# First MoE in three blocks of 768 tokens in place of six of 384, its sums packed into six PSUM banks

## The chip, the cores and the metric

One core of a Trainium2 chip runs the whole program. TensorE (PE in the profile) multiplies matrices and writes its results into PSUM, a memory of eight banks of 512 float32 columns on 128 partitions; VectorE (DVE), ScalarE (ACT) and GpSimd (POOL) do the elementwise work, SyncE (SP) issues the transfers. POOL does not touch PSUM in this kernel. The metric is the device time of one launch in microseconds (us); what is compared is the median of several runs.

## What is computed

A block-causal attention over q, k, v (4 batches, 8 heads, 576 positions, 64 wide) gives x of 2304 tokens x 512. Two MoE layers follow, in float32:

```
h = x @ w_in                     # 512 -> 2048
x2 = (h * cos(h)) @ w_out        # 2048 -> 512, the first MoE

logits = x2 @ w_gate             # 8 experts
P = exp(logits - logits.max())
for _ in range(8):               # rows, then columns, normalized
    P /= P.sum(1, keepdims=True) + 1e-09
    P /= P.sum(0, keepdims=True) + 1e-09
    P *= N / E
out = sum over e of P[:, e] * (relu(x2 @ w1[e]) @ w2[e])   # 512 -> 1024 -> 512
```

## The kernel before

Every float32 operand x is split into a part that TensorE's fp32r format holds (`xh`, by a copy that rounds) and the rest (`xl`, by a subtraction); a product is three matmuls, high by high, high by low, low by high (`mm3`, L473). The order of the instructions is written out by hand: each engine runs its own instructions in the order in which the code emits them, and semaphores make one wait for another.

**First MoE, `moe1`.** A unit (L191) is a pair of a block of 384 tokens and one of 16 chunks `f` of 128 hidden columns: six blocks, 96 units. The weights of a chunk are 512 + 512 columns (`raw[f]`), and they are split anew for each unit: `wsplit(n, 0)` makes `jh`, `jl` of `w_in`, `wsplit(n, 1)` those of `w_out`, the high part on ACT (L65), the low on POOL (L68). `h_unit` issues the 12 hidden matmuls into a PSUM tile `h` (pool `psh`, three banks) and the DVE's range reduction `ki`, `r`; `sine` runs on ACT; `g_unit` multiplies on the DVE (`g`), copies on ACT (`hh`) and subtracts on the DVE (`hl`). `o_unit(n - 2)` issues the 12 output matmuls of the unit two back into four PSUM tiles `acc` (pool `psa`, four banks, 384 of 512 columns used) that add up over the 16 chunks. At the last chunk of a block, ACT copies each to `xh` (L704) and the DVE writes the rest to `xl` (L705).

Between the units other work is put in. In the first 16, three steps each of `conv_gen` convert the last of the weights (they come as float64; DVE L92, L111, L115, L122, ACT L98, L99, POOL L124), and `leftover` finishes the last head of the attention. After blocks 1 to 5 have begun, `logits` of the block before runs on TensorE (eight matmuls into the one bank of pool `psm`) and `logits_t` turns it. From unit 35 on, `tprep` (L590) makes sums and differences of x2 on the DVE, and `steps` prepares the second MoE's first weights in the last block.

**Second MoE.** 96 groups, each of 768 tokens and a pair of chunks of an expert. In a group, `open_group` starts products `hx` and `hy`, and the loop goes on with `hz` (pool `psh`) and six output tiles `y`, also called `acc`. A product named S2 adds onto `hx` once ACT has copied it to `c`. `gate(n)` runs the next n of the list `gating`: logits of block 5, its turning, the maximum (`gmax`), `start_p` with the exponential, and eight column steps `cols`, each a matmul on sums and nine small DVE operations. P is first wanted at the second expert, in group 5.

Of the kernel before, what the change touches and what calls it, by code (L numbers as in the profile page):

```python
# [22 lines left out]
NC = DM // 128  # L23
# [17 lines left out]
def attention_moe_kernel(ctx: ExitStack, tc: tile.TileContext, qk, v, w_a, gate, w_b, out):  # L41
# [425 lines left out]
    with tc.manual_schedule():  # L467
        conv_gen, leftover = attention()
        psh = ctx.enter_context(tc.tile_pool(name="psh", bufs=3, space=PSUM))
        psa = ctx.enter_context(tc.tile_pool(name="psa", bufs=4, space=PSUM))  # L470
        psm = ctx.enter_context(tc.tile_pool(name="psm", bufs=1, space=PSUM))
# [6 lines left out]
        def hidden(wh, wl, blk):  # L478
            ps = psh.tile([128, TB], F32, tag="h", name="h")
            t0 = blk * TB  # L480
# [18 lines left out]
        def logits(blk):  # L499
            t0 = blk * TB  # L500
            ps = psm.tile([2 * NE, TB], F32, tag="m", name="plt")
# [6 lines left out]
        def logits_t(blk):  # L508
            ps = psm.tile([128, TT, 2 * NE], F32, tag="m", name="plg")
# [140 lines left out]
        def moe1():  # L650
            nonlocal th, tl
            with tc.tile_pool(name="m1", bufs=2) as p:
                wj, G = {}, {}
                units = [(blk, f) for blk in range(NB) for f in range(F1)]

                def hl_tiles():
                    return (p.tile([128, TB], F32R, tag="hh", name="hh", bufs=3),
                            p.tile([128, TB], F32R, tag="hl", name="hl", bufs=3))

                def wsplit(n, part, lo_eng=nc.gpsimd):  # L660
                    if 0 <= n < len(units):
                        hi = p.tile([128, DM], F32R, tag=f"jh{part}", name="jh", bufs=3 - part)
                        lo = p.tile([128, DM], F32R, tag=f"jl{part}", name="jl", bufs=3 - part)
# [3 lines left out]
                def h_unit(n):  # L667
                    ps = hidden(*wj.pop((n, 0)), units[n][0])
                    ki = p.tile([128, TB], I32, tag="ki", name="ki", bufs=1)
                    r = p.tile([128, TB], F32, tag="r", name="r")  # L670
                    g = p.tile([128, TB], F32, tag="g", name="g")
# [4 lines left out]
                    return ps, r, g  # L676

                def sine(ps, r, g):
                    nc.scalar.activation(r, r, AF.Sin, bias=half_pi)

                def g_unit(n, fill, ps, r, g):
                    fill[0]()
                    nc.vector.tensor_tensor(out=g, in0=ps, in1=r, op=ALU.mult)
                    G[n] = hl_tiles()
                    nc.scalar.activation(G[n][0], g, AF.Copy)  # L685
                    fill[1]()
                    nc.vector.tensor_tensor(out=G[n][1], in0=g, in1=G[n][0].bitcast(F32), op=ALU.subtract)  # L687
# [3 lines left out]
                def o_unit(n, between):  # L691
                    blk, f = units[n]
                    if f < F1 - 1:
                        between()
                    hh, hl = G.pop(n)
                    wh, wl = wj.pop((n, 1))
                    for m in range(NC):
                        if f == 0:
                            acc[m] = psa.tile([128, DM], F32, tag="a", name="acc")
                        s = slice(m * 128, (m + 1) * 128)  # L700
                        mm3(acc[m][:, 0:TB], wh[:, s], wl[:, s], hh, hl, f == 0, f == F1 - 1)
                        if f == F1 - 1:
                            cols = slice(blk * TB, (blk + 1) * TB)
                            nc.scalar.activation(xh[:, m, cols], acc[m][:, 0:TB], AF.Copy)  # L704
                            nc.vector.tensor_tensor(out=xl[:, m, cols], in0=acc[m][:, 0:TB],  # L705
                                                    in1=xh[:, m, cols].bitcast(F32), op=ALU.subtract)
                            if m == 1:
                                between()

                wsplit(0, 0, nc.vector)  # L710
                wsplit(1, 0, nc.vector)
                wsplit(0, 1)
                gate_prep()
                last = len(units) - F1
                none = lambda: None

                def some(n):
                    for _ in range(n):
# [5 lines left out]
                         13: lambda: w0.v(1, nc.vector), 14: lambda: wload(1)}  # L724
                tgen = None
                for n in range(len(units) + 2):
                    fill = [lambda: some(2), lambda: some(1)] if n < F1 else [none, none]
                    if n == 2 * F1 + 3:
# [3 lines left out]
                    if tgen and n % 2:  # L732
                        fill = [lambda: next(tgen, None), none]
                    between = none
                    if n < len(units):
                        hs = h_unit(n)
                        between = lambda: (sine(*hs), wsplit(n + 2, 0))
                    elif n == len(units) + 1:
                        open_group(0)
                    if n > 1:  # L740
                        o_unit(n - 2, between)
                    else:
                        between()
                    if n < len(units):
                        g_unit(n, fill, *hs)
                        wsplit(n + 1, 1)
# [207 lines left out]
```

## Time and profile before

| | us |
|---|---|
| runs | 2244.49, 2243.87, 2243.08 |
| median | 2243.87 |
| span of the profiled execution | 2242.3 |
| median above that span | 1.6 |
| TensorE busy in the span | 2158.4 (96%) |
| DVE / ACT / POOL busy | 1571.1 / 1020.5 / 1115.1 |
| first MoE: first hidden matmul to last output matmul | 269.3 to 712.0 |

The profile is of one execution. Its page gives busy times by engine and in 40 slices of the span; the trace behind it answers for stretches, lines, waits and single instructions. "PE" is the matmuls, "PEld" the loads of the stationary operand, which overlap them. A matmul's record is longer than the distance to the next one's start, since matmuls are pipelined; that distance is what counts.

### The profile page before, as it was taken

Reading aid. Unit: us, or ns where it says so; the run is one execution under the profiler, and the core shown is the slowest. Engines: PE = TensorE matmul, PEld = TensorE weight load, DVE = VectorE, ACT = ScalarE, POOL = GpSimd, SP = SyncE. Lnnn points to the kernel's source line nnn. Section 1 sums busy time; section 2 is a strip of 40 time slices with the busy share of each in tenths; the row PEclk is TensorE's granted clock in tenths of the full one; section 3 lists DMA queues with packets and bytes.
Section 4 is the critical chain, followed back from the end, with each engine's and each line's share of the span. In section 5 each row is a group of like instructions: output and inputs, shape, how many; then the busy total and the mean of one; then the engine's idle time right before and its main releaser. Section 6 shows DMA issues by size and latency. Waiting matters only on the chain.

```text
span 2242.3 us, 29534 instructions
## 1 busy us (share of the span) xinstructions
PE 2158.4 (96%) x10869; PEld 1910.0 (85%) x10869; DVE 1571.1 (70%) x2477; ACT 1020.5 (46%) x1882; POOL 1115.1 (50%) x928
## 2 busy tenths in 40 slices
PE   7888789999998999999999999999999999999999
PEld 4555589998997888888888888888988888888988
DVE  8888776676666876666676666666676666666665
ACT  5666655555555333433344333433444434333432
POOL 5888785665554334343554434343554434344341
PEclk9999999999999999999999999999999999999999
DMA  5666410000001112121221312121221312121220
GB/s 154 167 165 175 123 34 1 1 1 1 1 19 53 61 57 75 57 76 57 76 64 50 118 61 76 57 76 58 74 69 50 118 57 76 57 76 62 71 73 31
DMA packets 74160, 152.83 MB, mean 68 GB/s; under 512 B 32896, under 2 KB 32896, under 8 KB 74016
## 3 DMA queue, kind: packets, MB, share of 16 engines
q1 hardware_dynamic: 74016, 150.95, 21.7%
q8 instruction: 85, 1.39, 0.3%
q14 instruction: 59, 0.48, 0.1%
HBM read 136.91 MB, written 4.87 MB: 63 GB/s over the span
## 4 chain that ended last, share of the span: by engine, by line
PE 64%; DVE 3%; ACT 1%; issue 0%; ACTq 0%; DVEq 0%
PE acc L474 11%; PE acc L476 11%; PE acc L475 11%; PE hx L476 6%; PE hx L474 6%; PE hx L475 6%; PE hy L474 3%; PE hy L476 3%; PE hy L475 3%; PE hz L474 1%; PE hz L475 1%; PE hz L476 1%; DVE wal L576 0%; ACT hh L810 0%; DVE hl L811 0%; DVE tl L68 0%
## 5 line engine op out<-in xcount | busy, mean ns | idle before, releaser
L585 POOL TENSOR_TENSOR wv<-stg,wv 128x512 fp32r<-128x512 f32 x190 | 335.7, 1788 | 852.7 <-ACT wv L584 852.7
L474 PE MATMUL acc<-wv,hh 128*128 128x512 f32 x1152 | 456.3, 396 | 0.0
L476 PE MATMUL acc<-wv,hl 128*128 128x512 f32 x1152 | 455.6, 395 | 0.0
L475 PE MATMUL acc<-wv,hh 128*128 128x512 f32 x1152 | 454.5, 395 | 0.0
L839 DVE SCALAR_TENSOR_TENSOR oa<-acc,P,oa 128x512 f32<-128x512 f32 x540 | 379.0, 740 | 5.2 <-PE acc L476 4.3
L810 ACT ACTIVATE hh<-c 128x384 fp32r<-128x384 f32 x288 | 151.3, 525 | 409.6 <-DVE c L896 166.0
L68 POOL TENSOR_TENSOR jl<-raw,jh 128x512 fp32r<-128x512 f32 x190 | 253.5, 1344 | 168.5 <-ACT jh L65 166.5
L811 DVE SCALAR_TENSOR_TENSOR hl<-c,hh 128x384 fp32r<-128x384 f32 x288 | 163.9, 569 | 176.4 <-ACT hh L810 176.4
L476 PEld LDWEIGHTS acc<-wv,hl 128*128 128x128 f32 x1152 | 216.0, 187 | 53.7
L475 PEld LDWEIGHTS acc<-wv,hh 128*128 128x128 f32 x1152 | 215.9, 187 | 44.0
L474 PEld LDWEIGHTS acc<-wv,hh 128*128 128x128 f32 x1152 | 216.1, 188 | 43.0
L890 DVE TENSOR_TENSOR c<-hz,c 128x384 f32<-128x384 f32 x96 | 53.4, 556 | 192.0 <-PE hz L476 192.0
L880 ACT ACTIVATE c<-hx 128x384 f32<-128x384 f32 x96 | 47.4, 494 | 282.7 <-PE hx L476 282.7
L576 DVE TENSOR_TENSOR wal<-s,wah 128x1024 fp32r<-128x1024 f32 x96 | 172.2, 1793 | 0.0
L65 ACT ACTIVATE jh<-raw 128x512 fp32r<-128x512 f32 x192 | 119.3, 622 | 99.4 <-PE acc L475 86.7
L476 PE MATMUL h<-xh,jl 128*128 128x384 f32 x384 | 132.2, 344 | 10.3 <-POOL jl L68 10.2
L687 DVE TENSOR_TENSOR hl<-g,hh 128x384 fp32r<-128x384 f32 x96 | 100.7, 1048 | 56.8 <-ACT hh L685 56.8
L474 PE MATMUL h<-xh,jh 128*128 128x384 f32 x384 | 131.6, 343 | 9.1 <-ACT jh L65 8.9
L474 PE MATMUL acc<-hh,jh 128*128 128x384 f32 x384 | 129.4, 337 | 2.2 <-DVE xl L705 1.3
L474 PE MATMUL hy<-xh,wah 128*128 128x384 f32 x384 | 129.2, 337 | 1.3 <-DVE c L896 1.3
L475 PE MATMUL h<-xl,jh 128*128 128x384 f32 x384 | 130.2, 339 | 0.0
L476 PE MATMUL hy<-xh,wal 128*128 128x384 f32 x384 | 129.1, 336 | 0.7 <-DVE wal L576 0.7
(214 smaller groups left out, 5158.4 us busy)
## 6 DMA issues: line engine op xcount, KB each, us to landing
stg<-in_w_b_dram SPq DMA_DIRECT2D x192, 512.0 KB
cw<-in_w_a_dram SPq DMA_DIRECT2D x32, 512.0 KB
st<-in_qk_dram SPq DMA_DIRECT2D x64, 144.0 KB
v<-in_v_dram SPq DMA_DIRECT2D x31, 160.0 KB
tt<-inv SPq DMA_DIRECT2D x32, 144.0 KB
out_dram<-oa SPq DMA_DIRECT2D x18, 256.0 KB
kb<-ka SPq DMA_DIRECT2D x31, 144.0 KB
qb<-qa SPq DMA_DIRECT2D x31, 144.0 KB
```

The costliest lines, as they stand in the source:

```text
L65: nc.scalar.activation(hi, src, AF.Copy)
L68: eng_lo.tensor_tensor(out=lo, in0=src, in1=hi.bitcast(F32), op=ALU.subtract)
L474: nc.tensor.matmul(ps, lh, rh, start=first, stop=False, skip_group_check=go_on)
L475: nc.tensor.matmul(ps, lh, rl, start=False, stop=False, skip_group_check=go_on)
L476: nc.tensor.matmul(ps, ll, rh, start=False, stop=last, skip_group_check=go_on)
L576: eng.tensor_tensor(out=self.al, in0=self.s, in1=self.ah.bitcast(F32), op=ALU.subtract)
L585: eng.tensor_tensor(out=t[:, DM:2 * DM], in0=src, in1=t[:, 0:DM].bitcast(F32), op=ALU.subtract)
L687: nc.vector.tensor_tensor(out=G[n][1], in0=g, in1=G[n][0].bitcast(F32), op=ALU.subtract)
L810: nc.scalar.activation(hh, src, AF.Relu)
L811: nc.vector.scalar_tensor_tensor(out=hl, in0=src, scalar=0.0, in1=hh.bitcast(F32), op0=ALU.max, op1=ALU.subtract)
L839: nc.vector.scalar_tensor_tensor(out=o, in0=acc, scalar=p, in1=o, op0=ALU.mult, op1=ALU.add)
L890: nc.vector.tensor_tensor(out=c[0], in0=z, in1=c[0], op=ALU.add)
```

## The change

The blocks of the first MoE become 768 tokens, so there are 48 units, and each split of a weight chunk serves two half-units of 384 tokens. The hidden matmuls stay 384 columns wide, 24 to a unit, in two PSUM tiles of a pool `psh` of two banks. The output sums of 4 x 768 columns lie in six banks: `PLACE` puts chunk 0 of a pair at bank 0 (512) and the first half of bank 1 (256), chunk 1 at the second half of bank 1 (256) and bank 2 (512). So the output matmuls are 512 and 256 columns wide, and their count and total of columns stay. They are of the unit one back, in two halves of 12; the evictions follow each half at a block's end. `logits` of four of the six old blocks run inside the stage, in a tile of `psh` between the two halves; those of the last two go to the second MoE's gating list, whose calls are placed anew. `tprep` starts at unit 21 of 48 and takes one step a unit. After the stage the six banks become `psm`, `psz` (for `hz`) and `psa`.

```diff
-        psh = ctx.enter_context(tc.tile_pool(name="psh", bufs=3, space=PSUM))
-        psa = ctx.enter_context(tc.tile_pool(name="psa", bufs=4, space=PSUM))
-        psm = ctx.enter_context(tc.tile_pool(name="psm", bufs=1, space=PSUM))
+        psh = ctx.enter_context(tc.tile_pool(name="psh", bufs=2, space=PSUM))
...
-                units = [(blk, f) for blk in range(NB) for f in range(F1)]
+                units = [(blk, f) for blk in range(N // HB) for f in range(F1)]
+                NU = len(units)
+                PLACE = [[(0, 0, 0, 512), (1, 0, 512, 256)], [(1, 256, 0, 256), (2, 0, 256, 512)]]
...
+                    for m in range(2):
+                        s = slice((2 * half + m) * 128, (2 * half + m + 1) * 128)
+                        for i, (w, h) in enumerate(((wh, hh), (wh, hl), (wl, hh))):
+                            for b, at, t0, w_ in PLACE[m]:
+                                nc.tensor.matmul(acc[half, b][:, at:at + w_], w[:, s], h[:, t0:t0 + w_],
...
+                for blk in range(N // HB - 1):
+                    for i, k in ((1, 2 * blk), (4, 2 * blk + 1)):
+                        steps[(blk + 1) * F1 + i - last] = lambda k=k: logits(k, psh, "h")
+                        steps[(blk + 1) * F1 + i + 1 - last] = lambda k=k: logits_t(k, psh, "h")
...
+                        pa = hidden(*w, t0)
+                        ra = reduce_h(pa)
+                        pb = hidden(*w, t0 + TB)
+                        sine(ra)
+                        wsplit(n + 1, 0)
+                        ga = times(pa, ra)
+                        g_hi(n, 0, ga)
+                        rb = reduce_h(pb)
+                        g_lo(n, 0, ga)
+                        wsplit(n, 1)
+                        sine(rb)
+                        some(2)
+                        gb = times(pb, rb)
+                        g_hi(n, 1, gb)
+                        some(1)
+                        g_lo(n, 1, gb)
+                    else:
+                        open_group(0)
+                    if n:
+                        o_part(n - 1, 0)
+                        evacuate(n - 1, 0)
+                    if n - last in steps:
+                        steps[n - last]()
+                    if n:
+                        o_part(n - 1, 1)
+                        evacuate(n - 1, 1)
...
-        gating = [lambda: logits(NB - 1), last_logits, gmax, start_p]
+        gating = [lambda: logits(NB - 2, psm, "m"), lambda: logits_t(NB - 2, psm, "m"),
+                  lambda: logits(NB - 1, psm, "m"), last_logits, gmax, start_p]
...
-                gate(1)
-                z = psh.tile([128, TB], F32, tag="h", name="hz")
+                if g:
+                    gate(1)
+                z = psz.tile([128, TB], F32, tag="z", name="hz")
                 product(g, z, "A12", "B21", True)
+                if g == 0:
+                    gate(1)
...
-            gate(0 if g else 1)
+            if g in (1, 2):
+                gate(1)
```

Three more `gate(1)` for group 0 follow S3, A22 and S4, and the last call, `gate(1 if g else 2)`, becomes `if g: gate(1)`.

The DVE's order in the first MoE, at one unit of the middle. Each row is a line of the kernel, the operation, its output and inputs, the output's size and the engines that it waits for. Before, a unit and the next one's first row:

```order
L672 TENSOR_SCALAR ki<-h 128x384 [waits PE_49]
L674 SCALAR_TENSOR_TENSOR r<-ki,h 128x384 [waits DVE_49]
L683 TENSOR_TENSOR g<-h,r 128x384 [waits Activation_49]
L687 TENSOR_TENSOR hl<-g,hh 128x384 [waits Activation_49]
L672 TENSOR_SCALAR ki<-h 128x384 [waits PE_49]
```

After, a unit of two halves:

```order
L667 TENSOR_SCALAR ki<-h 128x384 [waits PE_49]
L669 SCALAR_TENSOR_TENSOR r<-ki,h 128x384 [waits DVE_49]
L678 TENSOR_TENSOR g<-h,r 128x384 [waits Activation_49]
L667 TENSOR_SCALAR ki<-h 128x384 [waits DVE_49,PE_49]
L669 SCALAR_TENSOR_TENSOR r<-ki,h 128x384 [waits DVE_49]
L686 TENSOR_TENSOR hl<-g,hh 128x384 [waits Activation_49]
L678 TENSOR_TENSOR g<-h,r 128x384 [waits Activation_49]
L686 TENSOR_TENSOR hl<-g,hh 128x384 [waits Activation_49]
```

The second half's `ki` and `r` stand between the first half's `g` and `hl`.

TensorE's output matmuls, the first ones of a unit. Before:

```order
L474 MATMUL acc<-hh,jh 128x384 [waits Activation_49]
L475 MATMUL acc<-hl,jh 128x384 [waits DVE_49]
L476 MATMUL acc<-hh,jl 128x384
L474 MATMUL acc<-hh,jh 128x384
L475 MATMUL acc<-hl,jh 128x384
```

After:

```order
L702 MATMUL acc<-hh,jh 128x512 [waits Activation_49]
L702 MATMUL acc<-hh,jh 128x256
L702 MATMUL acc<-hl,jh 128x512 [waits DVE_49]
L702 MATMUL acc<-hl,jh 128x256
L702 MATMUL acc<-hh,jl 128x512 [waits Pool_49]
L702 MATMUL acc<-hh,jl 128x256
L702 MATMUL acc<-hh,jh 128x256
L702 MATMUL acc<-hh,jh 128x512
```

Each stationary operand now serves two matmuls in a row, 512 and 256 columns wide.

ACT's order where the first MoE ends; `c<-hx` is the copy that the second MoE's first S2 waits for, `wbh` a weight split. Before:

```order
L704 ACTIVATE xh<-acc 128x384 [waits PE_49] x4
L880 ACTIVATE c<-hx 128x384
L560 ACTIVATE wbh<-stg 128x512 [waits DMAHW2_49]
L561 ACTIVATE wbh<-stg 128x256 [waits DMAHW3_49]
L885 ACTIVATE c<-hx 128x384 [waits DVE_49,PE_49,Pool_49]
```

After:

```order
L713 ACTIVATE xh<-acc 128x512 [waits PE_49]
L713 ACTIVATE xh<-acc 128x256 [waits PE_49]
L713 ACTIVATE xh<-acc 128x256 [waits DVE_49]
L713 ACTIVATE xh<-acc 128x512 [waits PE_49] x2
L713 ACTIVATE xh<-acc 128x256 [waits PE_49]
L713 ACTIVATE xh<-acc 128x256 [waits DVE_49]
L713 ACTIVATE xh<-acc 128x512 [waits PE_49]
L904 ACTIVATE c<-hx 128x384
```

Eight copies stand ahead of `c` in place of four, and the second 256-column piece of a bank waits for the DVE, which reads the first.

## Rows read from the trace of the kernel before

**Rows 1.** The page's first part: busy us (share of the span), instructions

```profile
PE 2158.4 (96%) x10869; PEld 1910.0 (85%) x10869; DVE 1571.1 (70%) x2477; ACT 1020.5 (46%) x1882; POOL 1115.1 (50%) x928
```

**Rows 2.** Stretches: length, busy us (count) PE, PEld, DVE, ACT, POOL; clock, DMA share, GB/s

```profile
269.30:346.50 77.20, 69.81 (x360) 66.70 (x361) 58.44 (x88) 42.80 (x74) 58.15 (x40) 0.92 0.11 32
346.50:485.80 139.30, 138.17 (x792) 134.93 (x792) 95.86 (x149) 76.00 (x137) 83.97 (x64) 1.00 0.00 1
485.80:629.70 143.90, 139.93 (x791) 134.59 (x791) 97.91 (x151) 77.40 (x139) 84.00 (x64) 1.00 0.00 1
629.70:707.70 78.00, 73.30 (x410) 69.37 (x409) 54.38 (x83) 40.95 (x74) 43.02 (x32) 1.00 0.13 41
744.80:797.80 53.00, 50.11 (x247) 43.08 (x246) 45.68 (x103) 18.75 (x36) 19.20 (x19) 1.00 0.20 60
797.80:813.50 15.70, 15.70 (x79) 14.07 (x78) 11.89 (x23) 6.25 (x12) 6.01 (x7) 1.00 0.22 65
```

**Rows 3.** Timeline (start, us, instruction): first and last of 25 matmul starts in a row

```profile
419.84 0.33 PE L474 MATMUL h<-xh,jh 128*128 128x384 f32 x1
...
424.00 0.33 PE L474 MATMUL h<-xh,jh 128*128 128x384 f32 x1
```

**Rows 4.** TensorE's waits in the first MoE: total us, times, longest

```profile
PE h L476 <- POOL jl L68: 10.2, 13, 2.4
PE h L474 <- ACT jh L65: 8.9, 4, 4.9
```

**Rows 5.** Timeline of the DVE in block 5: one unit, and a later `hl`

```profile
674.85 0.54 DVE L672 TENSOR_SCALAR ki<-h 128x384 int32<-128x384 f32 x1
...
676.73 0.56 DVE L683 TENSOR_TENSOR g<-h,r 128x384 f32<-128x384 f32 x1 [0.74 <-ACT r L679]
677.88 1.13 DVE L687 TENSOR_TENSOR hl<-g,hh 128x384 fp32r<-128x384 f32 x1 [0.59 <-ACT hh L685]
...
705.05 0.56 DVE L687 TENSOR_TENSOR hl<-g,hh 128x384 fp32r<-128x384 f32 x1 [0.59 <-ACT hh L685]
```

**Rows 6.** Groups on the DVE, 274 to 320 us, conversion (count, busy us, mean ns, idle before)

```profile
L122 DVE SCALAR_TENSOR_TENSOR tla<-cw,tla 128x512 int32<-128x512 int32 x6 | 6.8, 1126 | 0.0
L115 DVE SCALAR_TENSOR_TENSOR raw<-cw,raw 128x512 f32<-128x512 uint16 x5 | 5.6, 1119 | 0.1
...
L92 DVE TENSOR_SCALAR tla<-cw 128x512 int32<-128x512 int32 x5 | 4.0, 801 | 0.0
L111 DVE TENSOR_SCALAR raw<-cw 128x512 int32<-128x512 int32 x5 | 2.7, 533 | 0.0
```

**Rows 7.** Clock: two stretches as in rows 2, and the matmul after a gap

```profile
267.40:274.20 6.80, 4.90 (x15) 4.68 (x16) 3.47 (x7) 2.95 (x4) 2.47 (x2) 0.51 0.00 0
725.00:731.70 6.70, 6.23 (x20) 6.21 (x21) 2.90 (x8) 2.57 (x6) 5.50 (x6) 0.52 0.27 78
...
305.20 0.69 PE L474 MATMUL h<-xh,jh 128*128 128x384 f32 x1 [2.87 <-ACT jh L65]
```

**Rows 8.** Timeline of TensorE: 12 matmuls of 512 columns; two of 256, in the attention

```profile
999.69 0.39 PE L474 MATMUL acc<-wv,hh 128*128 128x512 f32 x1
...
1002.49 0.34 PE L474 MATMUL hx<-xh,wbh 128*128 128x384 f32 x1
...
182.04 0.28 PE L295 MATMUL sr<-qb,kb 128*128 128x256 f32 x1
...
182.28 0.31 PE L295 MATMUL sr<-qb,kb 128*128 128x320 f32 x1
```

**Rows 9.** Timeline, end of group 0: TensorE's wait, and `wal` on the DVE

```profile
725.47 0.58 PE L776 MATMUL pmb<-sm,ones 1*128 1x1 f32 x2 [3.26 <-DVE sm L772]
...
724.01 1.22 DVE L576 TENSOR_TENSOR wal<-s,wah 128x1024 fp32r<-128x1024 f32 x1
```

**Rows 10.** Timeline of TensorE where the first MoE ends: last output matmul, S2

```profile
711.66 0.34 PE L476 MATMUL acc<-hh,jl 128*128 128x384 f32 x1
712.96 0.44 PE L474 MATMUL hx<-th,wah 128*128 128x384 f32 x1 [0.96 <-ACT c L880]
```

More of the change, by code (lines that the diff above doesn't have):

```diff
@@ L689, in moe1, with g_hi, g_lo, o_part @@
+                def g_hi(n, k, g):
+                    nc.scalar.activation(G[n][0][:, k * TB:(k + 1) * TB], g, AF.Copy)
+                def g_lo(n, k, g):
+                    s = slice(k * TB, (k + 1) * TB)
+                    nc.vector.tensor_tensor(out=G[n][1][:, s], in0=g, in1=G[n][0][:, s].bitcast(F32),
+                                            op=ALU.subtract)
                 acc = {}
-                def o_unit(n, between):
+                def o_part(n, half):
                     blk, f = units[n]
[L693 to L708, printed above, removed]
@@ new lines, in o_part @@
+                    hh, hl = G[n]
+                    wh, wl = wj[n, 1]
+                    if f == 0:
+                        for b in range(3):
+                            acc[half, b] = pacc.tile([128, 512], F32, tag=f"a{half}{b}", name="acc")
+                    for m in range(2):
[3 more added lines that the diff above has]
+                                nc.tensor.matmul(acc[half, b][:, at:at + w_], w[:, s], h[:, t0:t0 + w_],
+                                                 start=f == 0 and i == 0 and at == 0, stop=f == F1 - 1 and i == 2,
+                                                 skip_group_check=True)
@@ new lines, in evacuate @@
+                def evacuate(n, half):
+                    blk, f = units[n]
+                    if f == F1 - 1:
+                        for m in range(2):
+                            for b, at, t0, w_ in PLACE[m]:
+                                cols = slice(blk * HB + t0, blk * HB + t0 + w_)
+                                c, src = 2 * half + m, acc[half, b][:, at:at + w_]
+                                nc.scalar.activation(xh[:, c, cols], src, AF.Copy)
+                                nc.vector.tensor_tensor(out=xl[:, c, cols], in0=src,
+                                                        in1=xh[:, c, cols].bitcast(F32), op=ALU.subtract)
@@ L710, in moe1 @@
                 wsplit(0, 0, nc.vector)
-                wsplit(1, 0, nc.vector)
-                wsplit(0, 1)
                 gate_prep()
-                last = len(units) - F1
-                none = lambda: None
+                last = NU - F1
                 def some(n):
@@ L748, in moe1 @@
                         leftover[n]()
-                    if n - last in steps:
-                        steps[n - last]()
-                    blk, f = divmod(n, F1)
-                    if blk and f == 4 and blk <= NB - 1:
-                        logits(blk - 1)
-                    if blk and f == 6 and blk <= NB - 1:
-                        logits_t(blk - 1)
         moe1()
+        psm = ctx.enter_context(tc.tile_pool(name="psm", bufs=1, space=PSUM))
+        psz = ctx.enter_context(tc.tile_pool(name="psz", bufs=1, space=PSUM))
@@ L760, in attention_moe_kernel @@
+        psa = ctx.enter_context(tc.tile_pool(name="psa", bufs=4, space=PSUM))
         fin = ctx.enter_context(tc.tile_pool(name="fin", bufs=1))
@@ L917, in attention_moe_kernel @@
                 w.v(0)
[L918 removed]
+            if g:
+                gate(1)
             ys(4)
```

76 lines of the change are left out of this document (33 added, 43 removed).

## The prediction

> **What bounds the kernel now.** I read the page's first part first: TensorE is busy 96% of a 2242.3 us span [rows 1], so only two things can change the time: what TensorE is given, and the few per cent in which it waits or runs slowly. Next I cut the first MoE at its blocks and the second at its first groups [rows 2]. A 384-column matmul starts every 173.3 ns when nothing is in its way (24 from 419.84 to 424.00 us, [rows 3]). Against that, block 0's 360 matmuls need 62.4 us and took 77.2: 14.8 lost. Blocks 1 to 4 have 392 each, 784 in a pair (135.9 us; the counts in the rows include some at the edges): 3.4 lost in blocks 1 and 2, 8.0 in 3 and 4. Block 5 has 404 (70.0): 8.0 lost. That is **34.2 us**. A group of the second MoE settles at 15.7 us; groups 2 to 4 took 53.0, 5.9 more than three of these [rows 2]; and group 0 ends in a wait of 3.26 us [rows 9], followed by half clock [rows 7].
>
> Who ends the waits in the first MoE: POOL's `jl` 10.2 us, ACT's `jh` 8.9 [rows 4]. But POOL and ACT are busy only half of the time [rows 1, 2], so I followed one unit on the DVE [rows 5]: `ki` to `g` 1.88 us (the sine lies between), `g` to `hl` 1.15 (ACT's copy lies between), `hl` 1.13: 4.16 us, against 24 x 0.1733 = 4.16 on TensorE. The chain has **no slack**, although the DVE idles 1.33 us of it. Whatever else stands in it (conversion in block 0, evictions, `tprep` in block 3, the second MoE's first weights in block 5) makes it late, ACT's sine late, and behind that sine `jh` and then `jl`. This is where the 34 us are lost.
>
> **The change, part by part.**
>
> *Two half-units share one chain.* A unit is now 24 hidden and 24 output matmuls, about 8.4 us. DVE's order is ki, r, g of half a, ki, r of half b, hl a, g b, hl b. With the steps of [rows 5], counted from the unit's first matmul: a's 12 matmuls end at 2.2 us, ki 2.3, r 2.9, g 4.1; ki b 4.6, r b 5.2, hl a 5.7 to 6.7 (POOL subtracting beside it), g b 6.7, hl b 7.8 to 8.4 (0.56, as at 705.05, where POOL rests). The next unit's first ki is due at 8.4 + 2.3 = 10.7. The DVE has **2.3 us to spare per unit** where it had none. `jl` for the next unit ends near 6.0 and is needed at 8.7; the PSUM buffer of half a is free at 4.7 and needed at 8.4, that of half b at 7.2 and 10.5. So two `psh` buffers do in the steady state.
>
> *Half the weight splits.* Half of POOL's and ACT's weight splits go. Neither engine bounds, so by itself this is worth nothing; but `hl` takes 1.13 where POOL subtracts beside it and 0.56 where it doesn't [rows 5], so the DVE's work gets shorter. SP's loads keep their order and have twice the time between.
>
> *Conversion.* Three steps still come with each of the first units, now every 8.4 us instead of 4.2. Four DVE operations cost 1.13, 1.12, 0.80 and 0.53 us in that stretch [rows 6] and make five steps: 3/5 x 3.58 = 2.1 us a unit, just inside 2.3. I leave 1.0 us lost (0 to 4). The ACT stall in front of a 2.9 us gap at 302, and the half clock that follows [rows 7], should go: POOL's two scalings there now lie in an idle stretch.
>
> *Start.* The first `jh` comes after the longest wait, 4.9 us [rows 4], which the change leaves alone, and 15 matmuls to 274.2 us run at half clock [rows 7]: 4.9 us for 2.6, so 2.3 remain. The second unit waits for `jl` as before and once for `g`: 1.2.
>
> *Matmuls cut at 512 and 256.* 576 pairs of (384, 384) become (512, 256). 512 columns: 2.80/12 = 233.3 ns [rows 8]; 256: 0.24/2 = 120 [rows 8], with some 5 ns either way between single starts. A pair costs 233.3 + 120.5 instead of 346.7: +7.1 ns, **+4.1 us** (1 to 7). The rows show 13 ns over the stream (160 ns at 2.4 GHz) at 384 columns and 20 at 512. The Trainium skill, page "TensorE: Matmul & The Clock Gate", section "Back-to-back issue gap", adds a fixed 2.5 ns to N/2.4 for every width: by it both pairs take 325 ns and the cut is free. The rows speak against that, and the sum goes by them.
>
> *Evictions in eight pieces.* At each of two inner block ends, ACT (from 7.7 us) and DVE work through eight pieces in turn. The two 256-wide pieces of a bank alternate between the engines, since the second copy waits for DVE's read of the first. With some 0.6 to 0.7 and 0.4 us for a 512- and a 256-wide piece on either engine (the 384-wide `g` takes 0.56, [rows 5]), DVE is done at 13.7 instead of 10.7: 3.0 late. The next unit's `logits` now take a `psh` buffer and want half a's: g ends at 4.7 + 3.0 = 7.7, TensorE arrives at 4.2 + 2.1 = 6.3. Lost: **1.5 us** after block 0; after block 1, where a `tprep` split follows the evictions (768 columns, twice 0.56 less some overhead), **2.6**. Four `logits` inside the stage cost up to 0.6 each beyond their matmuls, half of what block 1 loses: 2.4.
>
> *Last block.* Its steps, such as a `wal` of 1.22 us [rows 9], come once per 8.4 us and fit: 0.3.
>
> Sum for the first MoE: 2.3 + 1.2 + 1.0 + 4.1 + 1.5 + 2.6 + 2.4 + 0.3 = 15.4 where 34.2 were lost: **18.8 gained**.
>
> *Second MoE, groups 0 to 5.* (1) S2 overwrites what ACT's copy `c` must read first, and that copy stands behind the evictions: 1.30 us from the last `acc` matmul to S2 before [rows 10], about 2.9 after: -1.6. (2) `gmax` moves from the end of group 0 into group 1, which takes the 3.26 us wait away [rows 9]. What is late next is `wal`, which the DVE ends at 725.23 [rows 9]: S1 of group 1 needs it. I walked group 0 through: `A22` waits 0.8 for ACT's copy, the second `logits` 0.45 for the one `psm` buffer, S1 2.4 for `wal`. S1 of group 1 ended near 730.0 (half a us after the `pmb` row, then 12 matmuls at 0.32), 18.3 us after the last `acc`, with 9.7 of work in it; after, 17.5 with 11.1 of work (one `logits` more). Lost 8.6 before, 6.4 after, (1) included. (3) The column steps are DVE work; three come in group 2 and two in groups 3 and 4, where there were two in each of 1 to 4. Groups 2 to 4 overran by 5.9, group 1 by 1.1 after its S1 (744.8 - 730.0 against 15.7 - 2.1). Walked through with the new places, groups 1 to 5 lose 6.9, against 7.0. Together +2.3. The idle stretches near 2.5 us that I expect (block 2's first `logits`, S2, S1) lie between one of 2.4 [rows 4] and one of 2.87, which half clock followed (its record is twice as long, [rows 7]); block 0's mean clock of 0.92 [rows 2] has room for that fall and the one at the start alone. A fall costs about 3 us (20 matmuls at 0.32, [rows 7]); I charge 2 for the three places. `hz` in a bank of its own changes nothing: three tiles turned over three buffers before.
>
> Total: 18.8 + 2.3 - 2 = **19 us**. The profiled span of 2242.3 becomes 2223; the runs' median lies 1.6 above that span, so 2243.9 becomes **2225**.
>
> **The rivals.**
>
> *The waits return* (2231 to 2239, chance 0.20). Conversion at 2.1 us against 2.3 of slack is tight; if the DVE falls behind in block 0 (4 to 5 us) and the clock falls two or three times (3 us each), the gain is 19 - 12 = 7. For it: three idle stretches near 2.5 us. Against: DVE's operations are shorter once POOL rests.
>
> *Nothing is late* (2214 to 2221, chance 0.10). If evictions begin earlier than I drew and hide (4.1), conversion is free (1.0) and the clock holds (2): 26 us, 2218.
>
> *The cut is free* (2221, chance 0.03). If 512 and 256 columns both ran at the rate of the 384-column ones (231.1 and 115.6 ns), the 4.1 would go. The rows at 120 and 233 speak against it. The Trainium skill's formula, above, would have it so.
>
> *Slower: two buffers bind* (2245 to 2273, chance 0.07). Half b of a unit is read by `g` until 7.2 and its buffer is due at 10.5; a third one covered this. If each unit's DVE work grows by more than its 2.3 us of slack, TensorE waits in every one of 48 units. The gain is gone at 19/48 = 0.4 us a unit; 0.5 to 1 us would be 5 to 29 us slower. Both `hl` at the longer 1.13 would add only 0.5, conversion 2.1, so it takes both and more; and conversion ends with the ninth unit.
>
> *Slower: weight loads show* (2245 to 2255, 0.03). Each matmul has its own load of the stationary operand, which now gets 173 ns [rows 3]. If it needed them and could not begin before a 256-column matmul does, that one would last 173 instead of 120: 576 x 0.053 = 30 us, a net loss of 11; it decides from 153 ns on. In the attention two matmuls of 256 columns in a row took 120 [rows 8].
>
> **How the numbers follow.** Forecast 2225 (2220 to 2231): 0.52; waits return 0.20; nothing late 0.10; free cut 0.03; slower 0.10; 0.05 stays for a time within 0.2% (4.5 us, about what a measurement can tell from none) by causes I don't name, and 0.02 to 0.03 of the first rival's edge falls there too. The range 2214 to 2239 leaves out two in ten: the slower cases, the unchanged one and the edges. Faster 0.83, same 0.08, slower 0.09.
>
> **What would show it.** The first new block near 135 us (752 matmuls of the old cut, 130.3, and 4.5 lost) where blocks 0 and 1 took 146.4; no run of waits for `jl`; the DVE idle about 2 us before each unit's first ki outside conversion; pairs of 354 ns; a gap of 1.5 us before the first `logits` and 2.6 before the third; groups 2 to 4 still near 17 to 18 us. It is wrong if TensorE waits for `g` or `hl` in every unit, if 256-column matmuls take over 130 ns, or if the clock falls in block 1 or 2.

## The result, and the profile after

The changed kernel takes **2225.1 us** (median of 4 runs, 2224.4 to 2227.0) against 2244.2 beside it, a ratio of 0.9916 with a 95% interval of 0.9904 to 0.9929: 19 us faster. Its profiled execution spans 2222.6 us; the forecast was 2223 for the span and 2225 for the median. The sum came out, but not all of its terms, and one reason behind it was wrong: that halving the weight splits is worth nothing by itself.

The page's first part of after (columns as in [rows 1]):

```profile
PE 2147.9 (97%) x10869; PEld 1883.8 (85%) x10869; DVE 1531.4 (69%) x2476; ACT 964.1 (43%) x1786; POOL 997.1 (45%) x833
```

TensorE runs as many matmuls as before in 10 us less busy time, and POOL has 95 operations fewer, the low halves of the weight splits. The stretches, as in [rows 2]: the three blocks of 768 tokens, group 0 of the second MoE, and the half clock in group 0.

```profile
268.75:403.09 134.34, 132.31 (x745) 123.19 (x746) 94.55 (x155) 62.14 (x109) 60.97 (x42) 0.99 0.06 19
403.09:542.08 138.99, 137.99 (x792) 127.59 (x790) 85.89 (x152) 57.85 (x106) 45.80 (x32) 1.00 0.00 1
542.08:682.03 139.95, 137.95 (x792) 127.59 (x791) 84.58 (x154) 60.31 (x111) 44.58 (x31) 1.00 0.08 24
682.03:702.76 20.73, 17.28 (x90) 13.91 (x88) 9.19 (x19) 7.94 (x17) 2.82 (x4) 0.92 0.00 0
...
691.90:695.30 3.40, 3.40 (x12) 2.65 (x12) 0.00 (x0) 0.49 (x1) 0.00 (x0) 0.50 0.01 2
```

The first block takes 134.34 us where blocks 0 and 1 took 146.4; the clock is low for 3.4 us at its start, and the second fall of [rows 7] near 305 us is gone. TensorE's waits in the first MoE, which answer to [rows 4]:

```profile
PE h L472 <- ACT jh L65: 4.8, 1, 4.8
PE plt L500 <- DVE g L678: 3.0, 2, 2.0
PE h L472 <- DVE g L678: 1.4, 2, 0.9
PE h L474 <- POOL jl L68: 0.7, 1, 0.7
```

Only the first `jh`, ahead of the whole stage, is left of ACT's 8.9 us, and 0.7 of POOL's 10.2. After the second unit every unit takes 8.38 us, but for the four behind each block's end that hold `logits` or their turning. New are 1.4 us for `g` in the first two units and the two waits of `plt` (a matmul of `logits`) for a `psh` buffer. The timeline of TensorE at the first one (start, us, instruction, idle before):

```profile
418.90 0.35 PE L500 MATMUL plt<-xh,ghl 128*16 128x384 f32 x1 [1.00 <-DVE g L678]
```

The DVE ahead of it:

```profile
411.28 1.02 DVE L714 TENSOR_TENSOR xl<-acc,xh 128x512 fp32r<-128x512 f32 x2
412.75 2.11 DVE L714 TENSOR_TENSOR xl<-acc,xh 128x256 fp32r<-128x256 f32 x4 [0.45 <-ACT xh L713]
415.31 1.18 DVE L714 TENSOR_TENSOR xl<-acc,xh 128x256 fp32r<-128x256 f32 x2 [0.45 <-ACT xh L713]
416.41 0.55 DVE L667 TENSOR_SCALAR ki<-h 128x384 int32<-128x384 f32 x1
...
418.29 0.56 DVE L678 TENSOR_TENSOR g<-h,r 128x384 f32<-128x384 f32 x1 [0.74 <-ACT r L674]
```

The eight pieces of the eviction, in turn with ACT's, stand ahead of `ki` and `g`. TensorE's waits from 660 to 790 us, the edge to the second MoE and its first groups. The 3.26 us of [rows 9] are gone; S2's wait (`hx` for ACT's `c`) has grown from the 0.96 of [rows 10] to 2.44, and the column steps (`pcs`) wait 5.0 us, where they waited three times 0.66 or 0.67 before:

```profile
PE pcs L813 <- DVE sm L809: 5.0, 4, 1.9
PE hx L472 <- ACT c L904: 2.4, 1, 2.4
PE hy L474 <- DVE wal L573: 1.6, 1, 1.6
PE hx L472 <- ACT c L924: 0.7, 1, 0.7
```

### The profile page after: what moved, and what is told of

It reads as the page before. It is cut to its first block, busy times and chain, and to the rows that moved or that the text cites. A ratio compares the mean times of both kernels' runs of the same rounds, so it can differ in the third digit from the quotient of the medians.

```text
span 2222.6 us, 29515 instructions
## 1 busy us (share of the span) xinstructions
PE 2147.9 (97%) x10869; PEld 1883.8 (85%) x10869; DVE 1531.4 (69%) x2476; ACT 964.1 (43%) x1786; POOL 997.1 (45%) x833
## 4 chain that ended last, share of the span: by engine, by line
PE 82%; DVE 4%; ACT 1%; issue 0%; ACTq 0%; DVEq 0%
PE acc L472 12%; PE acc L474 11%; PE acc L473 11%; PE acc L702 8%; PE hx L474 6%; PE hx L472 6%; PE hx L473 6%; PE hy L474 3%; PE hy L472 3%; PE hy L473 3%; PE h L472 3%; PE h L474 3%; PE h L473 3%; PE hz L472 1%; PE hz L474 1%; PE hz L473 1%
## 5 line engine op out<-in xcount | busy, mean ns | idle before, releaser
L68 POOL TENSOR_TENSOR jl<-raw,jh 128x512 fp32r<-128x512 f32 x95 | 136.3, 1455 | 253.6 <-ACT jh L65 243.7
L674 ACT ACTIVATE r<-r,half_pi 128x384 f32<-128x384 f32 x96 | 59.2, 617 | 174.2 <-DVE r L669 173.7
L472 PE MATMUL hx<-th,wah 128*128 128x384 f32 x384 | 128.5, 335 | 2.4 <-ACT c L904 2.4
L474 PE MATMUL hx<-th,wal 128*128 128x384 f32 x384 | 128.7, 335 | 0.0
```

The source lines that it names most:

```text
L68: eng_lo.tensor_tensor(out=lo, in0=src, in1=hi.bitcast(F32), op=ALU.subtract)
L472: nc.tensor.matmul(ps, lh, rh, start=first, stop=False, skip_group_check=go_on)
L474: nc.tensor.matmul(ps, ll, rh, start=False, stop=last, skip_group_check=go_on)
```

## The experiments

Two reasons stood in the prediction: the DVE's order has no slack in a unit of 384 tokens and 2.3 us in one of 768 (theory 1); and the halved weight splits are worth nothing by themselves, which the rival denies (theory 2).

**1. One more DVE operation in each unit of before.**

```diff
                     nc.vector.tensor_tensor(out=G[n][1], in0=g, in1=G[n][0].bitcast(F32), op=ALU.subtract)
+                    nc.vector.tensor_tensor(out=r, in0=g, in1=g, op=ALU.add)
```

> The kernel before, with one more VectorE operation behind each unit's hl: a 128x384 sum into r, which nothing reads afterwards (about 0.56 us by the rows of g and r; 96 units, so 54 us of work on an engine that is idle a third of the time). Theory 1 (VectorE's order ki, r, g, hl has no slack in a unit of 384 tokens, and its length sets the unit): the whole price shows, 2280 to 2300 us. Theory 2 (the weight splits, on GpSimd and ScalarE, set the unit, and VectorE waits for them): VectorE has room, 2244 to 2255 us.

Measured: 2358.2 us, ratio 1.0505 (1.0489 to 1.0520), 114 us slower. The new operation's group on the DVE from 440 to 530 us (count, busy us, mean ns, idle before):

```profile
L688 DVE TENSOR_TENSOR r<-g 128x384 f32<-128x384 f32 x17 | 25.7, 1513 | 0.0
```

TensorE's waits in the stage:

```profile
PE h L476 <- POOL jl L68: 54.9, 77, 1.2
PE h L474 <- ACT jh L65: 18.4, 21, 5.1
```

No slack, as theory 1 says: a plain unit takes 5.56 us and not 4.16, so 1.40 of the operation's mean 1.51 us show. I had the price wrong: beside POOL's `jl` the operation takes 1.51 us and not 0.56. TensorE waits for the weight splits, which no edit touched; they are only late. From 440 to 530 us ACT idles 48.6 us ahead of its sines, for the DVE's `r`, and not at all ahead of the `jh` behind them. The releaser named by a wait is the last link of a chain.

**2. Half the weight splits in before, and POOL's part of that alone.** Chunks of odd `f` take the split tiles of the even one (first diff), or only its low half (second).

```diff
-                    if 0 <= n < len(units):
+                    if 0 <= n < len(units) and n % 2 == 0:
...
-                        wj[n, part] = (hi, lo)
+                        wj[n, part] = wj[n + 1, part] = (hi, lo)
```

```diff
+                        if n % 2 == 0:
+                            lo = p.tile([128, DM], F32R, tag=f"jl{part}", name="jl", bufs=3 - part)
+                            split(hi, lo, src, nc.scalar, lo_eng)
+                        else:
+                            lo = wj[n - 1, part, 0]
+                            nc.scalar.activation(hi, src, AF.Copy)
```

> The kernel before with half the weight splits and nothing else changed: units of odd f take the split tiles of the even f ahead of them, so the first MoE computes with the wrong weights there; the work on TensorE and VectorE is the same. Theory 1 (the unit is set by VectorE's order, the splits lie beside it): 2238 to 2246 us, 6 us less at most. Theory 2 (the splits set it: in the trace of before hl takes 0.96 us on average beside GpSimd's jl and 0.56 without, 0.4 us in each of 96 units, 38 us in all): half of that or more is gained, 2210 to 2229 us.

> The kernel before with GpSimd's half of the weight splits left out in units of odd f, which take the low halves of the even f ahead of them (so the first MoE computes with wrong low halves there); ScalarE still makes all the high halves. It parts what the run with half of all splits gained (18.5 us). Theory 2a (GpSimd's subtraction: its own 1.36 us that TensorE waits for, and VectorE's slower hl beside it): the gain stays, 2224 to 2228 us. Theory 2b (ScalarE's copies, queued ahead of the sine and of hh): it goes, 2239 to 2244 us.

Measured: 2225.2 us with half of all splits (ratio 0.9916, 0.9902 to 0.9931) and 2232.4 with half of POOL's (0.9950, 0.9935 to 0.9964). Theory 2 has the first: the halving alone gives 18.5 us, as much as the whole change, with six blocks and no longer units. **My "worth nothing" was wrong.** Of the second, neither 2a nor 2b has all: 12 us go with POOL's half alone, 6.6 more with ACT's. Of these 12, 1.2 lie behind the stage, in groups 0 and 1, where half clock lasts 3.4 us in this run and 6.8 in before. The stretches of the first (block 0; 1 and 2; 3 and 4; 5):

```profile
268.85:340.91 72.06, 66.92 (x361) 65.42 (x361) 53.92 (x89) 34.73 (x60) 37.35 (x26) 0.95 0.15 49
340.91:477.80 136.89, 136.89 (x791) 135.06 (x791) 89.33 (x149) 57.29 (x105) 41.28 (x32) 1.00 0.00 1
477.80:615.14 137.34, 137.17 (x791) 135.03 (x791) 88.14 (x149) 58.88 (x107) 41.31 (x32) 1.00 0.00 1
615.14:688.84 73.70, 71.66 (x408) 69.53 (x408) 48.81 (x81) 30.56 (x56) 20.99 (x15) 1.00 0.09 29
```

Block 3 alone, in the kernel before:

```profile
485.80:560.50 74.70, 71.00 (x396) 67.10 (x396) 51.00 (x79) 39.51 (x71) 42.88 (x32) 1.00 0.00 1
```

The same with half of POOL's splits:

```profile
481.24:554.32 73.08, 70.46 (x396) 67.17 (x396) 47.46 (x79) 39.14 (x71) 20.53 (x16) 1.00 0.00 1
```

And with half of all splits:

```profile
477.80:546.70 68.90, 68.73 (x397) 67.50 (x397) 45.42 (x77) 29.87 (x54) 20.68 (x16) 1.00 0.00 1
```

In block 3, where `tprep` runs, half of POOL's splits gives 1.6 us and ACT's half another 4.2. ACT's copy `th` for `tprep` stands behind the sine and a `jh` there, and the DVE's `tl`, queued ahead of `g`, waits for it: 2.00 us in before and with half of POOL's splits, 1.48 where no `jh` lies between. First before, then half of all splits:

```profile
535.56 1.42 DVE L68 TENSOR_TENSOR tl<-tt,th 128x768 fp32r<-128x768 f32 x1 [2.00 <-ACT th L65]
...
532.26 0.96 DVE L68 TENSOR_TENSOR tl<-tt,th 128x768 fp32r<-128x768 f32 x1 [1.48 <-ACT th L65]
```

Three such waits explain some of the 4.2 us; the rest is not itemized. Losses by the prediction's count (stretch less matmuls at 173.3 ns), us:

| kernel | block 0 | 1 and 2 | 3 and 4 | 5 | sum |
|---|---|---|---|---|---|
| before | 14.8 | 3.4 | 8.0 | 8.0 | 34.2 |
| half of POOL's splits | 10.8 | 2.8 | 6.3 | 3.8 | 23.7 |
| half of all splits | 9.7 | 1.0 | 1.4 | 3.7 | 15.8 |
| `hl` a unit later (3.) | 14.4 | 7.3 | 7.3 | 8.8 | 37.8 |

**3. The DVE's order relieved in before, splits unchanged.**

```diff
+                    low()
                     return ps, r, g
...
-                    nc.vector.tensor_tensor(out=G[n][1], in0=g, in1=G[n][0].bitcast(F32), op=ALU.subtract)
+                    late.append((n, g))
```

> The kernel before with one change in VectorE's order: hl of a unit is subtracted behind ki and r of the unit after it (ki, r, hl of the last, g), so that it no longer stands between g and the next ki. Six blocks of 384 tokens, as many weight splits as before, no cut matmuls. Theory 1 (the order has no slack): most of the 34 us that the first MoE lost are gained without the change itself, 2216 to 2230 us. Theory 2 (ScalarE's and GpSimd's splits set the unit, wherever hl stands): 2240 to 2250 us.

Measured: 2247.8 us, ratio 1.0019 (1.0010 to 1.0029), slower. Neither theory has it whole. The order did get slack (the DVE now waits 0.47 us for the hidden matmuls in a plain unit), but at each of five block ends the `hl` put off lands behind the evictions, and TensorE waits for it:

```profile
429.29 0.66 PE L475 MATMUL acc<-hl,jh 128*128 128x384 f32 x1 [2.03 <-DVE hl L686]
```

TensorE's waits in the stage, to be held against [rows 4]; the first kind was 0.2 us in before:

```profile
PE acc L475 <- DVE hl L686: 14.6, 9, 2.0
PE h L474 <- ACT jh L65: 8.2, 3, 5.2
PE h L476 <- POOL jl L68: 4.4, 6, 1.6
```

The unit at a block's end takes 6.49 us where it took 4.7, and behind two of the five waits half clock adds 1.5 each: some 12 us are the edit's own. An estimate without them, 37.8 less 12.1, is 25.7 us lost, so the slack gained 8.5 of the 34.2. It gained them by blocks. In block 3 the five units with `tprep` that took 4.85 to 5.29 us take 4.16 to 4.20, and the block is 3.9 us shorter in spite of its new wait:

```profile
488.90:559.76 70.86, 68.83 (x397) 67.41 (x397) 45.39 (x78) 38.70 (x71) 41.40 (x32) 1.00 0.00 1
```

In block 0 it gained 0.4 of 14.8: `jl` and `jh` stay late there. The order with `hl` put off, but ahead of the evictions at a block's end, was not run.

**4. Splits as often as before, in 14 units of after.** `again` splits both parts of the chunk a second time, into `th` and `tl`.

```diff
                         sine(rb)
+                        again(n, 0)
...
                         g_hi(n, 1, gb)
+                        again(n, 1)
```

> The kernel after, with the weights split as often as before in 14 units of the second block of 768 tokens (units 16 to 29): each unit splits both its parts a second time, on ScalarE and GpSimd, into the tiles th and tl, which nothing reads before they are overwritten. Theory 1 (two half-units on one VectorE order leave slack; how often the weights are split matters little): 2225 to 2228 us, and units 16 to 29 start 8.4 us apart as in after. Theory 2 (the halved splits bring the gain, 0.36 us for each 384 tokens): 14 x 0.72 = 10 us return, 2232 to 2237 us, and those units start 9.0 to 9.2 us apart.

Measured: 2229.0 us, ratio 0.9933 (0.9918 to 0.9948): 3 to 4 us return, not 10. The block with the doubled splits, to be held against the second stretch of after:

```profile
403.64:545.08 141.44, 138.74 (x791) 127.39 (x790) 108.49 (x151) 71.71 (x133) 85.28 (x60) 1.00 0.00 1
```

POOL works 39 us more, ACT 14, and the *same* DVE instructions take 22.6 us longer beside them; the block is 2.5 us longer. Plain units stay at 8.38; 1.0 of the 2.5 is at the block's edge, where the evictions are, the rest in units 29 to 31, where `tprep`'s last sums and first splits run. A fall of the clock behind the next `logits` costs 1.6 more, behind a wait of 2.0 us that after has too. So in plain units of 768 tokens the splits no longer set the time.

**5. Three more DVE operations in each unit of after.**

```diff
                         g_lo(n, 1, gb)
+                        for _ in range(3):
+                            nc.vector.tensor_tensor(out=rb, in0=gb, in1=gb, op=ALU.add)
```

> The kernel after with three more VectorE operations behind each unit's last hl: 128x384 sums into r, which nothing reads afterwards (by the run on the kernel before, where one such operation took 1.5 us beside GpSimd and 0.56 without: 2 to 3 us in a unit of 8.38). Theory 1 (a unit of 768 tokens has some 2 us of slack on VectorE): units 3 to 16 stay within 0.3 us of 8.38, and the eviction, the preparation of T1 to T4 and the start cost more, 2230 to 2250 us. Rival (after has no more slack in its order than before, where one operation per 384 tokens cost 114 us): 2 to 3 us in each of 48 units, 2320 to 2370 us.

Measured: 2246.0 us, ratio 1.0008 (0.9999 to 1.0018): 20 us for 144 operations where before paid 114 for 96. The new operation's group from 430 to 530 us:

```profile
L761 DVE TENSOR_TENSOR r<-g 128x384 f32<-128x384 f32 x33 | 18.4, 556 | 0.8
```

The three blocks of this run:

```profile
269.50:419.87 150.37, 138.07 (x744) 123.32 (x745) 122.31 (x201) 61.65 (x109) 61.04 (x42) 0.98 0.05 17
419.87:561.98 142.11, 139.54 (x792) 128.94 (x791) 110.52 (x201) 57.24 (x106) 45.91 (x32) 0.99 0.00 1
561.98:703.59 141.61, 138.04 (x791) 127.60 (x790) 109.26 (x203) 59.54 (x110) 44.53 (x31) 1.00 0.08 23
```

Plain units still take 8.38 us with 1.67 us more of DVE work: the slack is real. 16 of the 20 us are lost in the first block, where units with conversion take 9.9 to 10.6: there conversion had used most of it, and without that slack the first block loses what it had gained.

**6. The places where after still waits.** These are compared with after through their ratios to before; the first is after once more.

> The kernel after once more, as the measure for the three runs beside it: 2224 to 2227 us.

Measured: 2226.3 us, 0.9919 (0.9905 to 0.9933).

*The logits one unit later:*

```diff
-                    for i, k in ((1, 2 * blk), (4, 2 * blk + 1)):
+                    for i, k in ((2, 2 * blk), (5, 2 * blk + 1)):
...
-                        steps[(blk + 1) * F1 + i + 1 - last] = lambda k=k: logits_t(k, psh, "h")
+                        steps[(blk + 1) * F1 + i + (2 if i == 2 else 1) - last] = lambda k=k: logits_t(k, psh, "h")
```

> The kernel after with the logits of a finished block one unit later (third and sixth unit of the next block, not second and fifth; the first one's transposes two units behind it). Theory (the stalls of 1.0 and 2.0 us ahead of the first logits of a block come from VectorE, which is behind by the eviction of 768 tokens just then, and so gives back the PSUM buffer late): 2 to 3 us less than after, 2222 to 2223 us. Rival (the two PSUM buffers alone make the stall, at whatever unit a third user comes in): within 0.5 us of after, with the same stalls one unit later.

Measured: **2222.2 us**, ratio 0.9900 (0.9887 to 0.9914), 4 less than after beside it and the fastest version here. The second and third block:

```profile
403.15:541.02 137.87, 137.87 (x791) 127.53 (x790) 85.81 (x152) 57.87 (x106) 45.78 (x32) 1.00 0.00 1
541.02:679.89 138.87, 138.27 (x791) 127.54 (x790) 84.56 (x154) 60.33 (x111) 44.51 (x31) 1.00 0.08 24
```

Both stalls are gone, and each block is 1.1 us shorter; in the third a new wait of 0.6 us for `jl` takes back a part. The profiled spans of the two runs differ by 3.1 us: 2.1 lie in the blocks, 0.85 in the attention, which the edit doesn't touch. What makes the last of the 4 was not found. The two buffers bind only while the DVE is behind.

*Group 0's copy of `hx` ahead of the evictions:*

```diff
                         open_group(0)
+                        c0 = post.tile([128, TB], F32, tag="tt", name="c", bufs=3)
+                        nc.scalar.activation(c0, X[0], AF.Copy)
```

> The kernel after with one ScalarE instruction moved: group 0's copy of hx stands right behind the matmuls that open the group, ahead of the copies that evict the last block. Theory (the first S2 matmul, which writes into hx again, waits 2.44 us for that copy because it is queued behind the evictions, and the clock falls to half for 3.4 us behind it): both go, 3 to 4 us less than after, 2221 to 2222 us. Rival (the evictions that now come later hold up T2, the products after it or the buffers): 0 to 1 us less, with a new wait at A12 or S3.

Measured: 2226.1 us, 0.9917 (0.9904 to 0.9931), nothing gained. S2 no longer waits, but A12 does, for the last of the eviction:

```profile
693.61 0.44 PE L472 MATMUL hz<-xh,wbh 128*128 128x384 f32 x1 [1.72 <-DVE xl L714]
```

Group 0 takes 18.47 us where it takes 20.72 in after once more; 1.5 of the 2.25 is the half clock behind S2's wait, which is gone. But the clock fell at two other places, behind a `logits` stall of 2.0 us and behind S1's wait of 1.6 for `wal`, neither of which the edit touches, and each fall costs 1.5. The stretches:

```profile
559.80:563.20 3.40, 3.40 (x12) 2.12 (x11) 2.69 (x6) 2.71 (x5) 2.63 (x2) 0.50 0.00 0
706.60:710.00 3.40, 3.40 (x12) 3.21 (x13) 0.00 (x0) 0.36 (x2) 3.40 (x4) 0.50 0.35 92
```

*The column steps.* Three runs moved them: the extra one of group 2 dropped; with the later logits, all of them behind A12 and that one dropped; with the later logits, those of groups 2 to 4 among the output rows and one more behind the sixth row of group 2.

```diff
-            if g in (1, 2):
+            if g == 1:
                 gate(1)
```

```diff
-                if g:
-                    gate(1)
                 z = psz.tile([128, TB], F32, tag="z", name="hz")
                 product(g, z, "A12", "B21", True)
-                if g == 0:
-                    gate(1)
+                gate(1)
```

```diff
             ys(0)
+            if g > 1:
+                gate(1)
...
             ys(5)
+            if g == 2:
+                gate(1)
```

> The kernel after with one condition changed: the extra step of the gating behind the second output row stands in group 1 alone, and no longer in group 2, so that a column step of the normalisation always has half a group for its sums on VectorE; the last step comes half a group later. Theory (in groups 1 to 4 the matmul of a column step waits because it stands too close behind the sums of the step ahead: 1.74, 0.72, 1.86 and 0.66 us in the trace of after): 1 to 3 us less than after, 2222 to 2224 us. Rival (VectorE is late there whatever the distance, by its queue of output sums): within 0.5 us of after.

> The kernel after with the logits one unit later (the edit that measured 4 us less), and two edits on the gating: a column step in groups 1 on stands behind the A12 product and no longer ahead of it, which is six matmuls or 1.04 us later, and only group 1 has the extra step behind its second output row. Theory (those steps wait 0.66 to 1.86 us because they stand close behind the sums of the step ahead): of 5.0 us of such waits 0.7 to 1.5 are left, and the time is 3 to 4.5 us less than with the logits alone, 2217.5 to 2219.5 us. Rival (the step's VectorE operations, now later, hold up the first hidden block of the group and with it the output rows): the waits turn up at S3 or at the first rows, 2221 to 2224 us.

> The kernel after with the logits one unit later, and the column steps of groups 2 to 4 taken from the head of the group (ahead of A12) to two places among the output rows, behind the first and the fourth row, with one more behind the sixth row of group 2; group 1 stays as it is. Theory (in the traces so far a step at the head costs 1.6 to 2 us wherever it stands there, as a wait of its own matmul or, moved behind A12, as waits of hx and hy, because its ten small VectorE operations stand ahead of the additions on which ScalarE's copies and the next products wait; a step among the output rows costs 0.4 us): groups 2 to 4, which now lose 4.0, 3.3 and 2.0 us, lose 0.8 to 2 each, and the time is 4 to 6 us less than with the logits alone, 2216 to 2218.5 us. Rival (VectorE is the limit of these groups, so a step costs its 2.5 us of VectorE wherever it stands): 2221 to 2223 us, with waits at the steps among the rows.

Measured: 2225.8 us (0.9918, 0.9904 to 0.9931), 2222.5 (0.9905, 0.9890 to 0.9920) and 2225.6 (0.9918, 0.9904 to 0.9931): none gains. The first lowers the waits to 3.8 us. Group 3 takes 17.70 us, as before the change, and not 18.99, so the extra step was what cost it 1.3; group 5, where a step now falls, is 1.2 us longer. And in group 2 half clock follows the same wait of 1.74 us that it doesn't follow in after, which hides some 1.5 us:

```profile
729.10:732.50 3.40, 3.40 (x11) 3.02 (x10) 2.60 (x9) 0.84 (x2) 0.00 (x0) 0.50 0.00 0
```

Behind A12 the `pcs` waits drop to 0.8, and each step delays the products instead; two matmuls of group 3 in that run:

```profile
748.05 0.44 PE L472 MATMUL hx<-th,wbh 128*128 128x384 f32 x1 [0.70 <-ACT c L921]
...
749.67 0.45 PE L472 MATMUL hy<-xh,wah 128*128 128x384 f32 x1 [0.31 <-DVE c L922]
```

Among the rows two steps cost a group 0.7 us (group 4: 16.43 us, was 17.70), as its theory had it, and group 5, where steps now fall, 0.7 too; but the one behind the sixth row waited 5.67 us, because the DVE took up the step ahead of it only after `wal` and a row's sum, and half clock followed for 6.8 us. TensorE first:

```profile
743.23 0.59 PE L813 MATMUL pcs<-sm,ones 128*128 128x8 f32 x2 [5.67 <-DVE sm L809]
```

The DVE's timeline in that wait:

```profile
737.49 1.85 DVE L573 TENSOR_TENSOR wal<-s,wah 128x1024 fp32r<-128x1024 f32 x1
739.26 0.68 DVE L857 TENSOR_TENSOR oa<-acc,oa 128x512 f32<-128x512 f32 x1
739.86 0.15 DVE L814 TENSOR_SCALAR sm<-pcs 128x8 f32<-128x8 f32 x1
```

The same arrangement without that one step was not run.

## Why the prediction was right, and where it was not

*What bounds.* Right that the DVE's order had no slack (1.), and that a unit of 768 tokens has about the 2.3 us drawn: 1.67 more fit (5.). Wrong that this chain was the cause by itself, and that the halved splits are worth nothing. In block 3 either remedy removes the loss: half the splits (2.) and slack in the DVE's order (3.) both bring its units with `tprep` to 4.16 us or close to it. In block 0, half the splits takes 5.1 of 14.8 us, the slack 0.4, and neither reaches what after does there. In after the slack holds the loss off in the second block even with doubled splits (4.), and the first block needs it (5.). The change brings both remedies, and their gains don't add. Whether after's first block needs the halved splits too stays open: no buffer was free there for doubled ones.

*Terms of the first MoE*, forecast 15.4 us lost. From the first matmul to the last `acc` it took 442.4 us and takes 419.3; less 1.4 for the one `logits` that moved out, 21.6 are gained, so 12.6 are lost.

- Start and conversion 2.3 + 1.2 + 1.0: the first two units lost 2.3 and 2.2, conversion nothing. Same sum.
- Cut matmuls 4.1: a plain unit loses 0.06 us against 48 matmuls at 173.3 ns, 2.9 us in 48 units. Half of it is the cut: the 12 pairs take 4.19 us, 349.2 ns each, 2.5 more than two of 384. The other half lies in the first six hidden matmuls behind them, 0.03 us a unit; whether the cut causes that no run shows. The single starts, at 7.1 ns a pair, said too much. Starts of the hidden and the output matmuls of one unit, and of the next:

```profile
466.66 0.34 PE L472 MATMUL h<-xh,jh 128*128 128x384 f32 x1
...
470.85 0.51 PE L702 MATMUL acc<-hh,jh 128*128 128x512 f32 x2
...
475.04 0.34 PE L472 MATMUL h<-xh,jh 128*128 128x384 f32 x1
```

- Stalls 1.5 and 2.6: 1.0 and 2.0, for the reason given. Logits 2.4: 2.3. Last block 0.3: nothing.

*Second MoE.* S2 starts 2.84 us after the last `acc` (forecast 2.9), `A22` waits 0.71 (0.8), the `logits` 0.31 (0.45), S1 1.61 (2.4). One fall of the clock, 10 matmuls at 0.32 us and not 0.173, costs 1.5 (2 charged). From the last `acc` to S1's end it took 18.3 us and takes 19.1, with 1.4 more of work: 0.6 gained, where 2.2 less the 2 for the clock were forecast.

*The step that failed* is (3), the column steps: "groups 1 to 5 lose 6.9, against 7.0". From S1's end to group 5 they lose 10.1, 3.2 more than forecast. Nearly all of the 3.1 over before is in the waits of `pcs` for the sums of the step ahead, 5.0 us where it was 2.0: 1.74 and 0.72 in group 2, which has three steps, 1.86 in group 3, 0.66 in group 4. I walked the steps by their matmuls and single DVE operations and left out that a step's nine small DVE operations (2.3 to 3.1 us) queue behind `wal` and the rows' sums, so that a third step in one group makes the next ones late. Group 2 takes 19.75 us and group 3 19.03, against 17.67 before; without the third step group 3 is back at 17.70 (6.).

In the sum, 2.8 us more gained in the first MoE and 0.4 more around group 0 than forecast cancel 3.2 more lost here; the attention, which nothing touched, ended half a microsecond earlier. The forecast was nearer than its terms, and that is luck.

*The rivals.* No run of waits came back in the first block. Of "nothing is late" only the conversion came true. Two buffers bind only behind an eviction (6.). No weight load shows: the 256-column matmuls of the unit above start the next one 112 to 120 ns later. The free cut is nearer to the truth than its 0.03: 2.5 ns a pair.

## What to carry to other kernels

When TensorE waits for a side task (here a weight split), ask what that task is queued behind, and test both remedies alone, less of the side task and more slack around it; the share of an engine's time decides neither. Read such a test unit by unit: the moved `hl` of experiment 3 made the kernel slower as a whole and still removed the loss in block 3. An added operation must be priced at the place where it lands: the same DVE sum took 0.56 us alone and 1.51 beside GpSimd. Before a step is moved out of one wait, list what is queued behind it on each engine at its new place.

## What the runs showed of the hardware

The same 128x384 sum on VectorE took 556 ns in after (5.) and 1513 ns in before (1.), where GpSimd was subtracting beside it; 22.6 us of VectorE's time in one block came from doubled work on GpSimd and ScalarE (4.). In both kernels `ki`, `r` and `g`, which read `h` from PSUM, stay at 0.55 to 0.56 us beside GpSimd; only operations with both operands in SBUF lengthen (`hl` 0.56 to 1.13, [rows 5]). In the run of 1. the added sum takes 1.64 us where it starts 0.38 us behind a `jl`, and ends 0.41 us behind that `jl`'s end (at 450.12 us, for one); where it starts 0.09 us ahead of a `jl` it takes 0.55 (at 468.07). The Trainium skill has a rule for this ("SBUF — State Buffer", section "Who interferes with whom"): a VectorE instruction with two SBUF inputs contends with a GpSimd one that reads SBUF, for ports that only one of them can hold. The rows agree. Weighed in time, the rule would have warned that the sum of experiment 1 could cost more than its 0.56 us.

Half clock came in stretches of 3.4 or 6.8 us, at a granted clock of 0.50. It followed S2's idle 2.44 us in after, but not the same 2.44 us in the run of 5. It stayed away behind the 2.0 us ahead of after's third `logits`, and even behind 3.57 us at that place in the run of 5., but followed the same 2.0 in the runs of 4. and of the copy moved ahead. So whether an idle stretch of this length costs 1.5 us more differs from run to run.
